# Another order for the first steps of a gated-recurrence and SiLU-layer kernel on one core

## The chip, the cores and the metric

The kernel runs on one core of a Trainium2 chip. The metric is device time in microseconds (us) of one execution. The core has a matrix engine (PE; its weight loads are listed as PEld), three engines for elementwise work (DVE, the vector engine; ACT, the scalar engine; POOL, the general one) and SP, which here only sends DMA requests. Each engine runs its own instructions in the order of the program. Requests can also be sent from ACT and POOL. In the profile, SPq, ACTq and POOLq are these requests.

## The reference

Four sequences of 768 tokens, 8 heads of 48 values. Each head keeps a 48 x 48 state, which decays by a gate and takes up one outer product per token. All heads of a token together (384 values) then go through a layer of 2048 hidden values with SiLU.

```python
f = 1.0 / (1.0 + np.exp(-f_logit))
for t in range(S):
    state = f[:, :, t, :, None] * state + np.einsum('bhd,bhe->bhde', k[:, :, t], v[:, :, t])
    y[:, :, t] = np.einsum('bhd,bhde->bhe', q[:, :, t], state)
x = y.transpose(0, 2, 1, 3).reshape(B * S, H * D)
h = x @ w_in
out = (h * (1.0 / (1.0 + np.exp(-h)))) @ w_out
```

q, k, v and f_logit come in float32, [4, 8, 768, 48]; w_in is [384, 2048] and w_out [2048, 384].

## The kernel before

A sequence is cut into 6 chunks of 128 tokens. Within a chunk the recurrence becomes matrix products: the logarithms of the gates are summed along the tokens, q and k are scaled by exponentials of these sums, their products (scores) are masked and multiplied with v, and the state from the chunk before is added. Two chunks make a *pair*, which shares its loads and its pass through the SiLU layer. Pairs 0 to 3 hold the first two chunks of sequences 0 to 3 (form "T", with even and odd tokens interleaved); pairs 4 to 11 hold the later chunks.

There is no loop over the pairs. A string, `PLAN` (lines 39 to 105), lists all steps as `name.pair.part:engine:buffers`, and lines 483 to 487 emit them in that order. Each engine so works through its own steps in the order of the string and waits where an input or a buffer isn't ready. Buffers are numbered by hand: a step that takes a buffer waits until the last reader of what was in it is done. The names, with the lines that emit them:

- `f`, `k`, `q`, `v` (line 228): a load of 384 KB, or two of 192 KB as for `f.1`.
- `E` (234) and `L` (238): exponential and logarithm of the gates of a pair, on ACT.
- `cs` (305, 309): sums of the logarithms along the tokens, on PE. Those of part 1 end with eight small products (309) for the decay of the state.
- `ia`, `a` (317): the two exponentials that scale k and q, on ACT; `al` (256): the decay of the state.
- `ki`, `qg` (322): k and q times these, on DVE (V) or POOL (G).
- `tq` (329) and `qkc` (184, 182): transposes on PE, and their copy out of PSUM.
- `sc` (346) and `at` (354): scores, and their masking on DVE.
- `vb`: v cast to bf16. `d` (275), `sd`, `su` (393): the new state; `su` is on POOL.
- `y` (263), `yi` (362), `yc`, `yT` (374), `xc`: the output, its copy, its transpose and the copy into the layer's input.
- `mi` (249), `si` (254), `mo` (286), `oc`, `so`: first product, SiLU, second product, copy out, store. One `mi` is six products of 256 columns, one `mo` step four of 384.
- `wi` (207), `wo` (210): a quarter of w_in or w_out, requested from POOL and cast on its way.
- `idle.N.K` (436): K products of a zeroed tile, N columns each. Nothing reads them.

Ahead of the plan's other steps lines 454 to 457 put the first four loads, and then ACT's first table load:

```python
        loads = [t for t in plan if t[0] in SRC][:4]
        for t in loads:
            run(*t)
        nc.scalar.preload_act_table_set(TABLES["exp"])
```

Before, these four are `f.1.0`, `f.1.1`, `f.0.0` and `k.1.0`. `f.1.1` is the one load of the opening that is sent from ACT. Pair 1 goes first, pair 0 second, and their `mi` and `mo` steps follow; pair 2's recurrence is worked in between the `mo` steps.

Of the kernel before, what the change touches and what calls it, by code (L numbers as in the profile page):

```python
# [36 lines left out]


PLAN = """
f.1.0:S:0 f.1.1:A: E.1.0:A:0 L.1.0:A:0 idle.512.10::0 cs.1.1:P:0 f.0.0:S:1 E.0.0:A:1 k.1.0:S:0 L.0.0:A:1 idle.512.1::1 cs.1.0:P:1  # L40
q.1.0:S:0 idle.512.2::2 cs.0.0:P:2 idle.256.1::3 cs.0.1:P:3 a.1.1:A:0 qg.1.1:V:0 a.1.0:A:1 ia.1.1:A:2 ki.1.1:V: idle.512.1::4 tq.1.1:P:4 ia.1.0:A:3
ki.1.0:V:1 v.1.0:S:0 f.2.0:S:0 qg.1.0:V: idle.512.3::5 tq.1.0:P:1 vb.1.1:V:0 vb.1.0:G:1 d.1:P:5,6 qkc.1.1:V:0 qkc.1.0:V: idle.512.1::7 idle.256.1::7
sc.1.0:P:1,4 ia.0.0:A:0 k.0.0:S:1 ki.0.0:V:0 at.1.0.0:V:0 at.1.0.1:V: idle.512.2::7 idle.256.1::7 sc.1.1:P:7,1 at.1.1.0:V:1 at.1.1.1:V: a.0.1:A:2
ia.0.1:A:3 sd.1.0:A:0 wi.1:G: al.1:A:0 E.2.0:A:1 L.2.0:A:1 q.0.0:S:1 a.0.0:A:1 qg.0.0:V: idle.512.1::5 cs.2.0:P:0 cs.2.1:P:5 al.2:A:1 ia.2.1:A:0
su.1.0:G:0 ia.2.0:A:4 al.0:A:2 a.2.0:A:1 qg.0.1:V:1 idle.512.2::2 y.1:P:1,7 tq.0.0:P:4 v.0.0:S:1 yc.1.0:V:0 a.2.1:A:2 qkc.0.0:A:1 sd.1.1:V:0 wi.3:G:
ki.0.1:G: tq.0.1:P:3 qkc.0.1:V: yT.1.0:P:1 yi.1.1:P: yc.1.1:A:0 wi.0:G: idle.512.2::2 sc.0.1:P:3,4 vb.0.1:G:0 at.0.1.0:V:0 yT.1.1:P:7 xc.1.0:A:0
sc.0.0:P:6,5 at.0.0.1:V:1 at.0.0.0:V: vb.0.0:A:1 wi.2:G: idle.512.1::2 d.0:P:3,1 xc.1.1:A: sd.0.0:A:1 su.0.0:G:0 mi.1.2:P:7 mi.1.3:P:3 at.0.1.1:V:
y.0:P:4,6 q.2.0:S:0 yc.0.0:A:0 yi.0.1:P: wo.0:G: mi.1.6:P:5 yT.0.0:P:4 sd.0.1:V:1 su.0.1:G:0 xc.0.0:A:1 wo.1:G: yc.0.1:V:1 yT.0.1:P:6 xc.0.1:V:
qg.2.1:G:0 mi.1.7:P:1 k.2.0:S:0 si.1.7:A:0 mi.0.3:P:6 mi.0.7:P:4 wo.2:G: si.1.6:A: mi.0.6:P:0 mi.0.1:P:1 si.0.1:A:1 wo.3:G: su.1.1:G:0 si.0.6:A:
mi.0.0:P:5 mi.0.2:P:2 si.0.2:A: mi.1.0:P:1 ki.2.1:V: si.1.3:A: mi.1.4:P:0 si.1.4:A: si.0.0:A: si.1.2:A: mi.0.5:P:2 mi.1.5:P:3 si.0.5:A: mi.0.4:P:0  # L50
mi.1.1:P:7 mo.0.1.0:P:2 v.2.0:S:0 si.1.5:A: mo.0.0.0:P:3 si.1.0:A: si.1.1:A: mo.1.0.0:P:7 mo.1.1.0:P:1 mo.1.0.1:P: mo.1.1.1:P: qg.2.0:V:1 f.3.0:S:0
si.0.3:A: mo.0.1.1:P: si.0.7:A: ki.2.0:V: tq.2.0:P:4 qkc.2.0:V:1 tq.2.1:P:6 mo.0.0.1:P: si.0.4:A: qkc.2.1:V: mo.1.1.2:P: sc.2.1:P:6,4 sc.2.0:P:0,5
at.2.0.0:V:0 at.2.0.1:V: mo.1.0.2:P: mo.0.0.2:P: at.2.1.0:V:1 at.2.1.1:V: mo.0.1.2:P: mo.0.1.3:P: vb.2.0:G:0 vb.2.1:A:1 d.2:P:6,5 sd.2.0:V:0 E.3.0:A:1
L.3.0:A:1 y.2:P:4,0 mo.1.1.3:P: oc.0.1:V:0 mo.0.0.3:P: cs.3.0:P:2 f.5.0:S:1 E.5.0:A:0 L.5.0:A:0 yc.2.0:V:1 a.3.0:A:4 su.2.0:G:0 sd.2.1:V:0 q.5.0:S:0
yi.2.1:P: yc.2.1:A:0 yT.2.0:P:4 cs.3.1:P:6 al.3:A:0 ia.3.1:A:1 cs.5.0:P:5 xc.2.0:V:0 a.5.0:A:0 cs.5.1:P:0 k.3.0:S:0 ki.3.1:G:0 yT.2.1:P:4 xc.2.1:V:
oc.0.0:A:1 q.3.0:S:1 mo.1.0.3:P: oc.1.0:A:2 oc.1.1:V:3 qg.3.0:V:1 mi.2.6:P:4 al.5.1:A:2 qg.5.0:V:2 k.5.1:S:1 a.5.1:A:1 mi.2.0:P:1 mi.2.1:P:7
mi.2.2:P:3 q.5.1:S: qg.5.1:V:3 ia.5.1:A:2 al.5.0:A:3 a.3.1:A:4 qg.3.1:V: k.5.0:S: ia.5.0:A:0 ki.5.1:G: v.3.0:S:0 ia.3.0:A:1 ki.3.0:V: mi.2.5:P:5
tq.3.1:P:2 qkc.3.1:V:1 si.2.1:A:0 ki.5.0:G: si.2.2:A: si.2.0:A: su.2.1:G:0 mi.2.3:P:6 tq.3.0:P:0 si.2.3:A: mi.2.4:P:2 qkc.3.0:V: mi.2.7:P:1
mo.2.1.0:P:6 mo.2.1.1:P: vb.3.1:G:0 si.2.4:A: vb.3.0:V:1 d.3:P:2,0 sd.3.0:V:0 su.3.0:G:0 si.2.5:A: v.5.0:S:1 si.2.6:A: sc.3.1:P:4,5 sc.3.0:P:3,7
at.3.0.0:V:0 si.2.7:A: mo.2.1.2:P: mo.2.1.3:P: vb.5.0:G:2 at.3.1.0:V:1 mo.2.0.0:P:3 mo.2.0.1:P: mo.2.0.2:P: f.4.0:S:1 E.4.0:A:0 sd.3.1:V:0 f.6.0:S:0  # L60
qkD.5.1:S:0 at.3.1.1:V: qkD.5.0:S:1 oc.2.1:A:4 L.4.0:A:0 cs.4.1:P:5 E.6.0:A:1 L.6.0:A:1 at.3.0.1:V: v.5.1:S: sc.5.0:P:7,6 y.3:P:0,4 sc.5.1:P:2,1
# [456 lines left out]
```

## Time and profile before

| | us |
|---|---|
| device time, median of three runs | 177.55 (177.32 to 177.99) |
| span of the profiled execution | 175.6 |
| first `mi` of the layer begins | 19.41 |

The time of the profiled execution is known by its span alone, from the first to the last instruction; it lies 1.95 us under the median of the three runs, which have the start and the end of an execution in them too. Times in views are counted from the start of the span. In a row of the timeline stand the start, the time from the first start to the last end of the group, the engine, the line, the operation with output and input, the count, and in brackets the idle time ahead of it with what ended it. Matmuls are pipelined: a group of them lasts longer than the time until the next one can begin.

### The profile page before, as it was taken

What the parts mean: (1) busy time and instruction counts of PE and PEld (TensorE: products, weight loads), DVE (VectorE), ACT (ScalarE), POOL (GpSimd) and SP (SyncE); (2) the same over time, 40 slices, a digit from 0 to 9 for tenths busy, and PEclk for the clock granted to TensorE, in tenths of its full rate; (3) what the DMA queues carried; (4) which work ended last, traced back from release to release, by engine and by line L of the source; (5) the groups of instructions that cost most, each with busy time, mean ns of one, the idle gap of its engine ahead of it and who ended that gap; (6) DMA issues with size and microseconds to landing.
All of it is one profiled execution on the core that took longest, in us unless ns stands there. A gap on an engine that the chain in (4) does not pass through costs nothing.

```text
span 175.6 us, 4754 instructions
## 1 busy us (share of the span) xinstructions
PE 169.4 (96%) x1927; PEld 125.2 (71%) x1930; DVE 81.2 (46%) x166; ACT 129.8 (74%) x239; POOL 61.2 (35%) x104
## 2 busy tenths in 40 slices
PE   6889999999999999999999999999999999999992
...
GB/s 146 320 325 265 211 216 201 188 182 240 232 172 164 210 208 158 228 183 217 128 230 166 143 236 158 205 188 231 225 128 183 193 191 230 54 61 118 90 4 90
DMA packets 110677, 32.12 MB, mean 183 GB/s; under 512 B 104096, under 2 KB 110528, under 8 KB 110656
## 3 DMA queue, kind: packets, MB, share of 16 engines
...
## 4 chain that ended last, share of the span: by engine, by line
PE 79%; ACT 11%; DVE 5%; DMA 2%; issue 2%
PE pb L286 35%; PE pb L249 29%; ACT x L317 3%; ACT hT L254 3%; PE pb L350 3%; ACT L485 2%; DVE qk L322 2%; DMA f<-in_f_logit_dram 2%; PE pb L362 2%; PE pb L366 2%; PE pb L346 1%; PE pb L312 1%; PE pb L383 1%; PE pb L374 1%; DVE atm L354 1%
## 5 line engine op out<-in xcount | busy, mean ns | idle before, releaser
L249 PE MATMUL pb<-xT,w_in_sb 128*128 128x256 bf16 x576 | 69.1, 272 | 0.3 <-ACT hT L254 0.2
L286 PE MATMUL pb<-w_out_sb,hT 128*128 128x384 bf16 (+2 forms) x400 | 68.6, 320 | 0.0
L249 PEld LDWEIGHTS <-w_in_sb 128*128 128x128 bf16 x576 | 54.8, 98 | 9.0 <-issue 0.8
L254 ACT ACTIVATE hT<-pb 128x512 bf16<-128x512 f32 x96 | 50.5, 611 | 10.9 <-PE pb L249 10.7
L286 PEld LDWEIGHTS <-hT 128*128 128x128 bf16 x400 | 37.2, 98 | 20.5 <-issue 0.2
L393 POOL TENSOR_TENSOR st<-sd,al 48x192 bf16<-48x192 f32 x40 | 21.4, 535 | 59.0 <-PE pb L362 33.4
L354 DVE TENSOR_TENSOR atm<-pb,triu 128x512 bf16<-128x512 f32 x32 | 20.1, 684 | 11.2 <-PE pb L350 6.6
L317 ACT ACTIVATE x<-pb 128x384 f32<-128x384 f32 x48 | 21.0, 501 | 5.4 <-PE pb L305 3.0
L485 ACT ACT_TABLE_LOAD x17 | 21.8, 1283 | 0.3
L184 DVE COPY ob<-pb 128x384 f32<-128x384 f32 (+1 forms) x11 | 5.7, 528 | 27.3 <-PE pb L286 27.3
L387 DVE TENSOR_TENSOR sd<-pb,st 128x384 f32<-128x384 f32 x16 | 8.8, 552 | 11.8 <-PE pb L383 10.3
L322 POOL TENSOR_TENSOR qk<-q,x 128x384 bf16<-128x384 f32 x11 | 10.9, 996 | 9.0 <-ACT x L317 6.1
L322 POOL TENSOR_TENSOR qk<-k,x 128x384 bf16<-128x384 f32 x11 | 11.8, 1081 | 5.7 <-ACT x L317 2.4
L182 ACT COPY ob<-pb 128x384 f32<-128x384 f32 (+1 forms) x14 | 6.7, 477 | 8.5 <-PE pb L286 8.1
L234 ACT ACTIVATE e<-f 128x768 f32<-128x768 f32 x12 | 10.1, 840 | 3.8 <-DMA f<-in_f_logit_dram 3.7
L322 DVE TENSOR_TENSOR qk<-q,x 128x384 bf16<-128x384 f32 x13 | 8.2, 648 | 7.2 <-ACT x L317 7.1
L354 DVE TENSOR_TENSOR atm<-pb,mask 128x512 bf16<-128x512 f32 x16 | 10.1, 684 | 1.6 <-issue 1.0
L436 PE MATMUL pb<-zero,triu 128*128 128x512 bf16 (+1 forms) x26 | 9.0, 449 | 1.4 <-POOL triu masks.py:66 1.4
L184 DVE CAST yb<-pb 128x384 bf16<-128x384 f32 x14 | 7.6, 554 | 5.1 <-PE pb L366 2.6
L184 DVE COPY qkTT<-pb 128x1024 bf16<-128x1024 bf16 x7 | 4.6, 683 | 11.0 <-PE pb L329 11.0
L322 DVE TENSOR_TENSOR qk<-k,x 128x384 bf16<-128x384 f32 x13 | 9.0, 707 | 1.0 <-DMA k<-in_k_dram 0.8
L184 POOL CAST vb<-v 128x384 bf16<-128x384 f32 x12 | 6.4, 535 | 8.0 <-DMA v<-in_v_dram 7.7
...
## 6 DMA issues: line engine op xcount, KB each, us to landing
f<-in_f_logit_dram SPq DMA_DIRECT2D x11, 384.0 KB, 5.1
k<-in_k_dram SPq DMA_DIRECT2D x10, 384.0 KB, 5.5
q<-in_q_dram SPq DMA_DIRECT2D x10, 384.0 KB, 5.4
v<-in_v_dram SPq DMA_DIRECT2D x10, 384.0 KB, 4.9
...
w_in_sb<-in_moe_w_in_dram POOLq DMA_DIRECT2D x4, 384.0 KB, 8.6
w_out_sb<-in_moe_w_out_dram POOLq DMA_DIRECT2D x4, 384.0 KB, 10.5
...
```

The lines of the kernel that those rows point to most:

```text
L184: ENG[eng].tensor_copy(dst, src)
L234: return nc.scalar.activation(e, at("f", P)[:, j * w:(j + 1) * w], AF.Exp, scale=-1.0)
L249: nc.tensor.matmul(h[:, i, cols], w_in_sb[:, kk, n * 128:(n + 1) * 128], at("xT", P)[:, kk, cols], start=(kk == 0), stop=(kk == KT - 1))
L254: return nc.scalar.activation(at("hT", P)[:, 2 * j:2 * j + 2, :], at("h", P, j).rearrange("p (n c) -> p n c", n=2), AF.Silu)
L286: nc.tensor.matmul(at("o" + key, P, i)[:, 0:cols.stop - cols.start], at("hT", P)[:, n, i * C:(i + 1) * C], w_out_sb[:, n, cols], start=(n ...
L317: nc.scalar.activation(at(kind, P, i).rearrange("p h d -> p (h d)"), at("cs", P, i)[:, 0:HD], AF.Exp, scale=1.0 if kind == "ia" else -1.0)
L322: ENG[eng].tensor_mul(at("qk", P, i)[:, j, :, 0:D], heads("qk"[j], P, i), at("ia" if j else "a", P, i))
L354: ENG[eng].tensor_mul(at("atm", P, i)[:, r], at(f"s{r}", P, i).rearrange("p (n c) -> p n c", c=C), mask[:, None, :].to_broadcast([C, NP, C]))
L387: nc.vector.tensor_add(at("sd", P, i), d_ps, prev_state(P, i))
L393: nc.gpsimd.tensor_mul(at("st", P, i)[lo:lo + D, :, r * D:(r + 1) * D], at("sd", P, i)[lo:lo + D, :, r * D:(r + 1) * D], al_of(P, i)[lo:lo ...
L436: nc.tensor.matmul(buf["pb", int(got)][:, 0:rest[0]], triu, zero[:, 0:rest[0]], start=True, stop=True, skip_group_check=True)
L485: nc.scalar.preload_act_table_set(turns[n])
```

## The change

Only the string is changed; every step is still there, with the same operands. Up to `cs.3.0` the order, some engines and many buffer numbers are others; behind it the order is as it was but for `k.3.0`, `su.0.1` and a few buffers. Three numbers count for all of the opening: the fillers before are ten of 512 columns at the very start and 16 more in thirteen places; after it there are seven and a half behind `cs.1.1`, a half one ahead of `sc.1.0` and ten behind `sc.1.1`.

```diff
-f.1.0:S:0 f.1.1:A: E.1.0:A:0 L.1.0:A:0 idle.512.10::0 cs.1.1:P:0 f.0.0:S:1 E.0.0:A:1 k.1.0:S:0 L.0.0:A:1 idle.512.1::1 cs.1.0:P:1
-q.1.0:S:0 idle.512.2::2 cs.0.0:P:2 idle.256.1::3 cs.0.1:P:3 a.1.1:A:0 qg.1.1:V:0 a.1.0:A:1 ia.1.1:A:2 ki.1.1:V: idle.512.1::4 tq.1.1:P:4 ia.1.0:A:3
-ki.1.0:V:1 v.1.0:S:0 f.2.0:S:0 qg.1.0:V: idle.512.3::5 tq.1.0:P:1 vb.1.1:V:0 vb.1.0:G:1 d.1:P:5,6 qkc.1.1:V:0 qkc.1.0:V: idle.512.1::7 idle.256.1::7
-sc.1.0:P:1,4 ia.0.0:A:0 k.0.0:S:1 ki.0.0:V:0 at.1.0.0:V:0 at.1.0.1:V: idle.512.2::7 idle.256.1::7 sc.1.1:P:7,1 at.1.1.0:V:1 at.1.1.1:V: a.0.1:A:2
-ia.0.1:A:3 sd.1.0:A:0 wi.1:G: al.1:A:0 E.2.0:A:1 L.2.0:A:1 q.0.0:S:1 a.0.0:A:1 qg.0.0:V: idle.512.1::5 cs.2.0:P:0 cs.2.1:P:5 al.2:A:1 ia.2.1:A:0
-su.1.0:G:0 ia.2.0:A:4 al.0:A:2 a.2.0:A:1 qg.0.1:V:1 idle.512.2::2 y.1:P:1,7 tq.0.0:P:4 v.0.0:S:1 yc.1.0:V:0 a.2.1:A:2 qkc.0.0:A:1 sd.1.1:V:0 wi.3:G:
-ki.0.1:G: tq.0.1:P:3 qkc.0.1:V: yT.1.0:P:1 yi.1.1:P: yc.1.1:A:0 wi.0:G: idle.512.2::2 sc.0.1:P:3,4 vb.0.1:G:0 at.0.1.0:V:0 yT.1.1:P:7 xc.1.0:A:0
-sc.0.0:P:6,5 at.0.0.1:V:1 at.0.0.0:V: vb.0.0:A:1 wi.2:G: idle.512.1::2 d.0:P:3,1 xc.1.1:A: sd.0.0:A:1 su.0.0:G:0 mi.1.2:P:7 mi.1.3:P:3 at.0.1.1:V:
-y.0:P:4,6 q.2.0:S:0 yc.0.0:A:0 yi.0.1:P: wo.0:G: mi.1.6:P:5 yT.0.0:P:4 sd.0.1:V:1 su.0.1:G:0 xc.0.0:A:1 wo.1:G: yc.0.1:V:1 yT.0.1:P:6 xc.0.1:V:
-qg.2.1:G:0 mi.1.7:P:1 k.2.0:S:0 si.1.7:A:0 mi.0.3:P:6 mi.0.7:P:4 wo.2:G: si.1.6:A: mi.0.6:P:0 mi.0.1:P:1 si.0.1:A:1 wo.3:G: su.1.1:G:0 si.0.6:A:
...
+f.1.0:S:0 f.0.0:S:2 k.1.0:S:0 q.1.0:S:1 f.1.1:A: E.1.0:A:0 L.1.0:A:2 cs.1.0:P:1 E.0.0:A:0 ia.1.0:A:2 v.1.0:S:5 k.0.0:S:3 cs.1.1:P:4 f.2.0:S:0
+ki.1.0:V:3 ia.1.1:A:3 a.1.1:A:4 L.0.0:A:2 al.1:A:3 a.1.0:A:2 ki.1.1:V:4 idle.512.7::0 idle.256.1::0 cs.0.0:P:0 vb.1.0:G:2 qg.1.1:V: tq.1.1:P:2
+q.0.0:S:0 cs.0.1:P:1 a.0.0:A:3 ia.0.0:A:4 vb.1.1:A:1 al.0:A:4 qg.1.0:V: qkc.1.1:V:0 tq.1.0:P:7 d.1:P:4,0 qkc.1.0:V: idle.256.1::3 sc.1.0:P:3,2 wi.1:G:
+ki.0.0:V:3 sc.1.1:P:7,5 a.0.1:A:0 sd.1.0:A:0 at.1.0.1:V:1 at.1.0.0:V: idle.512.10::6 at.1.1.0:V:2 ia.0.1:A:4 at.1.1.1:V: E.2.0:A:0 L.2.0:A:0
+cs.2.1:P:3 wi.3:G: qg.0.0:V: su.1.0:G:0 a.2.1:A:1 sd.1.1:V:0 wi.0:G: al.2:A:0 ia.2.1:A:3 y.1:P:1,6 yi.1.1:P: tq.0.0:P:5 cs.2.0:P:2 ki.0.1:G:2
+qg.0.1:G: tq.0.1:P:4 yc.1.1:A:1 v.0.0:S:2 yc.1.0:V:0 yT.1.0:P:0 vb.0.1:G:5 qkc.0.0:V:0 vb.0.0:G:1 yT.1.1:P:6 wi.2:G: wo.0:G: ia.2.0:A:4 a.2.0:A:0
+d.0:P:3,7 xc.1.1:A:1 qkc.0.1:V: xc.1.0:V: sc.0.1:P:5,2 at.0.1.0:V:3 sc.0.0:P:6,1 sd.0.0:A:1 at.0.0.1:V:2 su.0.0:G:0 mi.1.3:P:4 mi.1.2:P:5 mi.1.6:P:0
+mi.1.7:P:3 at.0.1.1:V: at.0.0.0:V: y.0:P:1,2 yi.0.1:P: sd.0.1:V:1 yc.0.1:V:0 q.2.0:S:0 si.1.6:A:0 mi.1.0:P:6 k.2.0:S:0 yc.0.0:A:2 yT.0.0:P:1
+xc.0.0:A:2 f.3.0:S:0 yT.0.1:P:0 xc.0.1:V: si.1.7:A: mi.1.1:P:2 qg.2.0:G:2 qg.2.1:G:1 v.2.0:S:3 mi.0.2:P:7 mi.0.0:P:0 ki.2.1:V: si.1.3:A: si.1.1:A:
+mi.0.6:P:1 si.0.0:A:2 si.1.2:A: wo.1:G: si.0.2:A: mi.0.1:P:3 si.0.1:A: mi.0.5:P:2 mi.0.7:P:4 si.0.6:A: si.0.7:A: si.1.0:A: si.0.5:A: mi.0.4:P:3
+mi.0.3:P:1 mi.1.4:P:5 mo.0.1.0:P:4 wo.2:G: si.0.4:A: wo.3:G: si.1.4:A: tq.2.1:P:6 mo.1.1.0:P:7 ki.2.0:V: tq.2.0:P:2 mo.1.0.0:P:3 si.0.3:A: mi.1.5:P:5
...
+mo.1.1.2:P: cs.3.0:P:2 f.5.0:S:0 E.5.0:A:0 L.5.0:A:0 yc.2.0:V:1 a.3.0:A:4 mo.0.1.3:P: mo.1.1.3:P: oc.0.1:V:0 mo.0.0.3:P: su.2.0:G:0 sd.2.1:V:0
```

What it does to each engine's own order:

- **First loads.** The first four loads of the string are now `f.1.0`, `f.0.0`, `k.1.0` and `q.1.0`, all sent from SP. `f.1.1` is the fifth, so ACT's program has the table load ahead of it.
- **ACT.** `ia.1.0`, `ia.1.1` and `a.1.1` come ahead of `L.0.0`; before, `E.0.0` and `L.0.0` came first. `vb.1.1` comes to ACT from DVE, and `qkc.0.0`, `vb.0.0` and `xc.1.0` leave ACT.
- **PE.** `cs.1.0` and `cs.1.1` come first, with no filler ahead of them. Two half-pairs of scores (`sc.1.0` and `sc.1.1`) stand beside each other, and four `mi` steps ahead of `y.0` where there were two.
- **POOL.** `wi.1` and `wi.3` are requested together ahead of `su.1.0`; `qg.0.1` and `vb.0.0` come to POOL; both halves of `qg.2` stand ahead of `wo.1`; `su.0.1` moves behind `ki.5.1`.
- **SP.** `q.2.0` takes the buffer of `q.0.0` and so waits for `qg.0.0` and `qg.0.1`; `k.2.0`, `f.3.0` and all later loads stand behind it. `f.5.0` takes the buffer of `f.3.0` and waits for `E.3.0`.

More of the change, by code (lines that the diff above doesn't have):

```diff
@@ L48 @@
-y.0:P:4,6 q.2.0:S:0 yc.0.0:A:0 yi.0.1:P: wo.0:G: mi.1.6:P:5 yT.0.0:P:4 sd.0.1:V:1 su.0.1:G:0 xc.0.0:A:1 wo.1:G: yc.0.1:V:1 yT.0.1:P:6 xc.0.1:V:
-qg.2.1:G:0 mi.1.7:P:1 k.2.0:S:0 si.1.7:A:0 mi.0.3:P:6 mi.0.7:P:4 wo.2:G: si.1.6:A: mi.0.6:P:0 mi.0.1:P:1 si.0.1:A:1 wo.3:G: su.1.1:G:0 si.0.6:A:
-mi.0.0:P:5 mi.0.2:P:2 si.0.2:A: mi.1.0:P:1 ki.2.1:V: si.1.3:A: mi.1.4:P:0 si.1.4:A: si.0.0:A: si.1.2:A: mi.0.5:P:2 mi.1.5:P:3 si.0.5:A: mi.0.4:P:0
-mi.1.1:P:7 mo.0.1.0:P:2 v.2.0:S:0 si.1.5:A: mo.0.0.0:P:3 si.1.0:A: si.1.1:A: mo.1.0.0:P:7 mo.1.1.0:P:1 mo.1.0.1:P: mo.1.1.1:P: qg.2.0:V:1 f.3.0:S:0
@@ L52 @@
[L52 to L55, printed above, removed]
```

13 lines of the change are left out of this document (8 added, 5 removed).

## The prediction, made ahead of the result

> **What bounds the kernel now.** I read the page first: the share of each engine, the slices, the chain that ended last.
>
> ```profile
> span 175.6 us, 4754 instructions
> PE 169.4 (96%) x1927; PEld 125.2 (71%) x1930; DVE 81.2 (46%) x166; ACT 129.8 (74%) x239; POOL 61.2 (35%) x104
> PE   6889999999999999999999999999999999999992
> PE 79%; ACT 11%; DVE 5%; DMA 2%; issue 2%
> ```
>
> PE is busy nearly everywhere and carries 79% of the chain; only the first slices are thinner. So I asked for the busy time by stages, and for the chain in order of time.
>
> ```profile
> 22.40:31.00 8.60, 8.60 (x83) 7.67 (x82) 2.58 (x4) 7.41 (x13) 5.37 (x9) 1.00 1.22 207
> 36.00:43.00 7.00, 7.00 (x123) 4.55 (x121) 5.01 (x9) 2.69 (x4) 0.53 (x2) 1.00 0.99 217
> ...
> 0.74 3.44 DMA f<-in_f_logit_dram
> 19.48 1.42 PE pb L249 x12
> 22.67 8.52 PE pb L249 x78
> 31.19 4.55 PE pb L286 x28
> ```
>
> From 22.4 us PE is full (8.60 of 8.60, then 7.00 of 7.00), and 13 `mi` steps (78 products in 8.52) make 0.655 each, without a gap. What PE has left from the first `mi` on is the same before and after: no product moves from one side of that point to the other. The end therefore moves by as much as the `mi` steps move, unless a gap opens later. The question is when PE comes to them.
>
> **The opening, term by term.** The timeline of the first microseconds has the durations.
>
> ```profile
> 0.74 0.47 ACTq L228 DMA_DIRECT2D f<-in_f_logit_dram  x1
> 0.74 1.00 SPq L228 DMA_DIRECT2D f<-in_f_logit_dram  x2
> 1.25 1.28 ACT L457 ACT_TABLE_LOAD   x1 [1.25 <-PEq L502]
> 1.37 4.07 PE L436 MATMUL pb<-zero,triu 128*128 128x512 bf16 x10 [1.37 <-POOL triu masks.py:66]
> 4.20 0.84 ACT L234 ACTIVATE e<-f 128x768 f32<-128x768 f32 x1 [1.67 <-DMA f<-in_f_logit_dram]
> 4.33 0.15 PEld L436 LDWEIGHTS <-triu 128*128 128x128 bf16 x1 [0.28 <-issue]
> 4.76 0.15 PEld L436 LDWEIGHTS <-triu 128*128 128x128 bf16 x1 [0.28 <-issue]
> 5.06 0.10 PEld L305 LDWEIGHTS <-tincl 128*128 128x128 bf16 x1 [0.15 <-issue]
> 5.08 0.84 ACT L238 ACTIVATE lf<-e 128x768 bf16<-128x768 f32 x1
> 5.97 0.48 PE L305 MATMUL pb<-lf,tincl 128*128 128x384 bf16 x2 [0.53 <-ACT lf L238]
> 6.29 0.34 PE L309 MATMUL pb<-halves,lf 128*128 128x2 bf16 x8
> 7.03 0.59 PE L436 MATMUL pb<-zero,triu 128*128 128x512 bf16 x2
> 7.43 2.41 ACT L317 ACTIVATE x<-pb 128x384 f32<-128x384 f32 x6
> 9.08 0.54 POOL L184 CAST vb<-v 128x384 bf16<-128x384 f32 x1 [5.17 <-DMA v<-in_v_dram]
> 9.56 0.91 POOL L207 DMA_DIRECT2D w_in_sb<-in_moe_w_in_dram  x1
> 10.55 0.62 PE L329 MATMUL pb<-ident,qk 128*128 128x128 bf16 x8 [0.41 <-ACT x L317]
> 10.69 1.28 DVE L184 COPY qkTT<-pb 128x1024 bf16<-128x1024 bf16 x2
> 12.48 2.48 DVE L354 TENSOR_TENSOR atm<-pb,mask 128x512 bf16<-128x512 f32 x4
> ```
>
> *`f.1.1`.* `E.1.0` needs both halves of `f.1`. The ACT half was requested at 0.74 and ended the wait at 4.20; the table load followed the request. Now the table load comes first. Bounds: the request goes out at about 0.8, if only the instruction stream is held, or at 0.74 + 1.28 = 2.02, if it waits for the table load to end; then all of the opening is 1.28 later. No row shows an ACT request behind unrelated ACT work. A POOL request waited so: `wi.1`, which needs nothing from `vb.1.0`, began at 9.56, as that copy ended at 9.62. But a POOL request takes 0.91 where ACT's took 0.47 and SP's 0.50 each, and SP has no datapath to wait for: ACT's is nearer to SP's. I take 0.8, so `E.1.0` at 4.20 as before, and keep 2.02 as a rival. The Trainium skill (Perfetto Trace Analysis, "DVE / Act Engine Instruction") says that the sequencer is free for the next instruction once it has pushed an ACT one into its wait queue. No row here tests that; by it the sum would be the one I take.
>
> *Decays first.* `L.1.0` ends at 5.92 as before. `E.0.0` now shares the buffer of `E.1.0` and runs from 5.95 to 6.8. The three exponentials ahead of `L.0.0` save pair 1 at most one logarithm, 0.84.
>
> *PE starts at half speed.* The ten fillers began 0.43 apart (weight loads at 4.33 and 4.76), two later ones 0.21 apart (0.59 less one's 0.38); the change came by 5.06, 3.7 after PE's first work. Without them `cs.1.0` is PE's first work, at 5.97, and by the same interval PE is slow until 9.65. `cs.1.0` and `cs.1.1` take 4 x 0.32 in place of 4 x 0.16. The eight small products hold PE 0.2 at full speed (6.29 to the next filler at 6.49); slow, between 0.4 (twice) and 1.2 (eight slow weight loads of 0.15), I take 0.6, nearer to the row that has just these. PE is through at 5.97 + 1.28 + 0.6 = 7.85. `ia.1.1` begins at about 8.1, `a.1.1` ends at 9.0, `L.0.0` at 9.75: the 0.84 is mostly spent on the wait for `cs.1.1`.
>
> *The fillers stand in line.* Seven and a half begin at 7.85: until 9.65 4.2 of them, then 3.3 x 0.21 = 0.7, to 10.35. `cs.0.0` (2 x 0.16), `tq.1.1` (0.45 until the next may begin), `cs.0.1` (0.32 + 0.2) and `tq.1.0` (0.62) end at 12.25; their inputs are there by then. Before, `tq.1.0` ended at 11.17: **1.1 later**.
>
> *Masks.* `qkc.1.0` 0.68 and the four masks, 2.48, stay, and `ki.0.0` (0.55) stands between them as before. The masks end at 16.0, against 14.96: 1.0 later. The ten fillers behind `sc.1.1` fill PE until about 15.9 and take 2.1 beside these masks; they cost nothing as long as the masks end last.
>
> ```profile
> 12.30 1.08 POOL L393 TENSOR_TENSOR st<-sd,al 48x192 bf16<-48x192 f32 x2 [1.83 <-ACT al L256]
> 13.33 0.81 POOL L207 DMA_DIRECT2D w_in_sb<-in_moe_w_in_dram  x1
> 14.21 0.99 POOL L322 TENSOR_TENSOR qk<-k,x 128x384 bf16<-128x384 f32 x1
> 15.24 0.58 PE L263 MATMUL pb<-vb,atm 64*128 64x48 bf16 x32
> 16.51 1.07 ACT L182 COPY qkTT<-pb 128x1024 bf16<-128x1024 bf16 x1
> 18.96 0.37 PEld L275 LDWEIGHTS <-qk 64*128 64x128 bf16 x16 [0.23 <-DVE atm L354]
> ```
>
> *From the masks to the first `mi`.* Before, this took 19.41 - 14.96 = 4.45: ACT's slow `qkc.0.0` (1.07) and three copies behind it held `d.0` until 18.96. Now these are spread over DVE and POOL. Two strings are left. On PE: `cs.2.1` 0.52 after the fillers, `y.1` 0.4, `yi.1.1` 0.2, `tq.0.0` 0.45, `cs.2.0` 0.32, `tq.0.1` 0.62, to 18.4. On POOL: `su.1.0` from 13.4 (1.08), the request `wi.0` 0.8, `ki.0.1` and `qg.0.1` 0.99 each, to 17.3, so inside the first. Then `qkc.0.1` 0.68 and the scores of pair 0, 0.44: `mi.1.3` begins at 19.55. The stretch is 0.9 shorter, against masks 1.0 later: **+0.15**.
>
> *The first `mi` steps.* Three steps took 22.67 - 19.41 = 3.26 with `y.0` and the transposes among them, where the work is 3.1: `y.0` had waited for the last mask. With four `mi` steps ahead of `y.0` (2.6) the masks of pair 0 (2.48) are hidden: **-0.15**. If they weren't, it would cost what is left of them, about 0.2.
>
> ```profile
> q<-in_q_dram SPq DMA_DIRECT2D x1, 384.0 KB, 7.8
> w_out_sb<-in_moe_w_out_dram POOLq DMA_DIRECT2D x1, 384.0 KB, 10.4
> ...
> 23.00 0.80 POOL L210 DMA_DIRECT2D w_out_sb<-in_moe_w_out_dram  x1
> 39.06 0.84 ACT L234 ACTIVATE e<-f 128x768 f32<-128x768 f32 x1 [2.03 <-DMA f<-in_f_logit_dram]
> 43.82 0.49 ACT L317 ACTIVATE x<-pb 128x384 f32<-128x384 f32 x1 [3.04 <-PE pb L305]
> ```
>
> *Transfers.* The first two rows are of the view of the DMAs; their last number is the time from request to landing, here of `q.2.0` and `wo.1`. `q.2.0` (7.8 to land) now goes out behind `qg.0.1`, near 17.4, and lands between 22 and 25. Nothing of pair 2 is wanted before `tq.2.1`, near 32. But `wo.1` now waits on POOL behind both `qg.2`: requested at 25 to 27 where it was at 23.00, it lands, at 10.4 or less, by 37.4 at the latest, and the fifth `mo`, right behind pair 2's scores, wants it near 36. I take nothing for it, as less traffic is in flight, and keep 1.5 as its price. `f.5.0` waits for `E.3.0` now; ACT had 3.04 spare ahead of `a.3.0`. `su.0.1` adds 1.08 to POOL near 48, ahead of `ki.5.0`, whose scores come ten microseconds later. I cost both at nothing.
>
> Sum: +0.15 - 0.15, and 0.1 for the waits between engines that I rounded away: 175.7 against the profiled 175.6. On the median of 177.55 that is **177.65**, no change.
>
> **The rivals.**
>
> *The request waits for the table load.* For it speaks `wi.1`; against it ACT's short request. All steps follow `E.1.0`, so 1.28 is added: **178.95**, slower. It decides from the point where `f.1.1`'s landing passes 4.2 by more than 0.8.
>
> *PE wakes late.* One interval, 3.7, is one sample. If PE is still slow at the end of the fillers, these take 0.5 longer, and `cs.0.0` to `tq.1.0` (1.9) up to as much again. The middle is 0.9: **178.55**. For it speaks that `cs.1.1` uses PE thinly; against it that ten plain fillers needed no more than 3.7. The Trainium skill (TensorE: Matmul & The Clock Gate, "What's actually happening") has a rule against this change: the clock opens after a busy window of 3413 ns that runs freely, not from the first product. As an estimate from that page, PE would open 3.4 to 6.8 after its start, and the middle, 5.1, would make the sum some 0.9 longer; the row's 3.7 lies inside.
>
> *The relief is larger than its price.* If PE is awake at `cs.1.0`, or the fillers end sooner, `tq.1.0` can end at 11.2 as before, and the shorter stretch of 3.55 behind the masks is a gain of 0.9 to 1.1: **176.55**. Against it stands that nothing runs on PE in its first 6 us.
>
> *`wo.1` is late*, as priced: **179.15**.
>
> **How the numbers follow.** My forecast 0.40, the request behind the table load 0.28, late waking 0.12, the larger relief 0.12, late `wo.1` 0.08. The forecast's own range is 177.1 to 178.3. The whole range, 176.8 to 179.4, takes in the table-load case and half of the others' tails. Half a per cent, 0.9, is about what a measurement of this kernel can tell from no change. Faster by more: most of the relief, 0.11. Slower: most of the table-load case and of late `wo.1`, half of late waking, 0.40. Within it: 0.49.
>
> **What would show it.** In the trace after, the ACT request begins at 0.8 (or at 2.0); `E.1.0` starts at 4.2 (5.5); the fillers behind `cs.1.1` run 0.43 apart and end near 10.4 (10.9 or more if PE wakes late); the masks of pair 1 end at 16.0; the first `mi` begins at 19.55, and PE shows no gap from there to 43. A gap ahead of an `mo` with a DMA as its releaser, or a first `mi` before 18.7 or after 20.4, would make the prediction wrong.

## The result and the profile after

Over 20 runs each, the changed kernel has a median of 178.62 us (177.15 to 179.81), the kernel before 177.26 (177.13 to 178.47). The ratio is 1.0058, with a 95% interval of 1.004 to 1.0075: slower, clear of noise, and just beyond the half per cent up to which the forecast called it no change. Ratios leave out the runs in which the chip was in a slower state; medians and ranges have all runs in them. 177.65 was forecast, within a range of 176.8 to 179.4; the range held, the likeliest case was about a microsecond too fast. Against its own base the miss is larger: the forecast added 0.1 to 177.55, the median of three runs, and the 20 runs of the kernel before have 177.26. The profiled execution had a span of 176.1, where the one before had 175.6. It took 177.90, so a time lies 1.8 above its span.

The page of the changed kernel, the lines that were shown of before:

```profile
span 176.1 us, 4727 instructions
PE 166.7 (95%) x1920; PEld 124.9 (71%) x1920; DVE 80.5 (46%) x165; ACT 129.3 (73%) x238; POOL 64.2 (36%) x106
PE   0699999999999999999999999999999999999992
PEclk9999999999999999999999999999999999999999
PE 88%; ACT 7%; DMA 2%; DVE 1%; issue 1%; ACTq 0%
```

Only the first three slices of PE differ: 0, 6 and 9 instead of 6, 8 and 8. PE's share of the chain has grown from 79% to 88%, which doesn't mean that PE does more, but that it now holds the opening too. The timeline of the opening (start, time, engine, line, operation, count, wait in brackets):

```profile
0.74 1.28 ACT L456 ACT_TABLE_LOAD   x1 [0.74 <-PEq L501]
0.77 0.48 ACTq L227 DMA_DIRECT2D f<-in_f_logit_dram  x1
4.27 0.84 ACT L233 ACTIVATE e<-f 128x768 f32<-128x768 f32 x1 [2.25 <-DMA f<-in_f_logit_dram]
6.04 0.48 PE L304 MATMUL pb<-lf,tincl 128*128 128x384 bf16 x1 [6.04 <-ACT lf L237]
7.53 3.36 PE L435 MATMUL pb<-zero,triu 128*128 128x512 bf16 x8
10.68 0.40 PE L304 MATMUL pb<-lf,tincl 128*128 128x384 bf16 x1
10.92 0.33 PE L304 MATMUL pb<-lf,tstrict 128*128 128x384 bf16 x1
12.06 0.61 PE L328 MATMUL pb<-ident,qk 128*128 128x128 bf16 x8
13.92 2.48 DVE L353 TENSOR_TENSOR atm<-pb,mask 128x512 bf16<-128x512 f32 x4
...
18.70 0.50 PE L373 MATMUL pb<-ident,yb 128*128 128x128 bf16 x6
19.13 0.51 PE L274 MATMUL pb<-vb,qk 64*128 64x96 bf16 x16
19.64 0.64 PE L345 MATMUL pb<-qkTT 48*64 48x128 bf16 x32
20.21 2.79 PE L248 MATMUL pb<-xT,w_in_sb 128*128 128x256 bf16 x24
```

How to read it: the request on ACT went out at 0.77, beside the table load that ran from 0.74 to 2.02. The Trainium skill (Perfetto Trace Analysis, "DVE / Act Engine Instruction") has the sequencer free for the next instruction once it has pushed one into the wait queue; this row agrees. All eight fillers of 7.53 ran at half speed (3.36 together, 0.43 apart); a sum of 384 columns took 0.48 at 6.04, 0.40 at 10.68 and 0.33 at 10.92, so PE reached full speed near 10.8. `tq.1.0` ended at 12.67, the masks at 16.40, and the first `mi` began at 20.21, 0.80 later than before (19.41). In the windows after it (us, PE's busy time with its count, granted clock, DMA share, GB/s), PE is as full as before, and nothing that was moved on the queues shows:

```profile
22.40:31.00 8.60, 8.60 (x113) 1.00 1.19 208
36.00:43.00 7.00, 7.00 (x93) 1.00 0.75 160
```

Of the 0.80, 0.5 is left at the end of the span (176.1 - 175.6); 0.13 of the rest is that PE rests less between 22 and 125 us (table below).

### The profile page after: what moved, and what is told of

It reads as the page before. It is cut to its first block, busy times and chain, and to the rows that moved or that the text cites. A ratio compares the mean times of both kernels' runs of the same rounds, so it can differ in the third digit from the quotient of the medians.

```text
span 176.1 us, 4727 instructions
## 1 busy us (share of the span) xinstructions
PE 166.7 (95%) x1920; PEld 124.9 (71%) x1920; DVE 80.5 (46%) x165; ACT 129.3 (73%) x238; POOL 64.2 (36%) x106
## 3 DMA queue, kind: packets, MB, share of 16 engines
q0 software_dynamic: 3936, 3.74, 12.4%
## 4 chain that ended last, share of the span: by engine, by line
PE 88%; ACT 7%; DMA 2%; DVE 1%; issue 1%; ACTq 0%
PE pb L285 35%; PE pb L248 31%; PE pb L435 3%; ACT hT L253 3%; PE pb L349 3%; PE pb L361 2%; ACT L484 2%; PE pb L328 2%; PE pb L304 2%; DMA f<-in_f_logit_dram 2%; PE pb L365 2%; PE pb L311 2%; PE pb L373 1%; PE pb L345 1%; PE pb L382 1%; PE pb L262 1%
## 5 line engine op out<-in xcount | busy, mean ns | idle before, releaser
L392 POOL TENSOR_TENSOR st<-sd,al 48x192 bf16<-48x192 f32 x40 | 22.2, 555 | 57.0 <-PE pb L361 33.8
L321 POOL TENSOR_TENSOR qk<-q,x 128x384 bf16<-128x384 f32 x13 | 13.5, 1047 | 9.7 <-DMA q<-in_q_dram 5.4
L386 DVE TENSOR_TENSOR sd<-pb,st 128x384 f32<-128x384 f32 x16 | 8.7, 551 | 10.8 <-PE pb L382 10.0
L321 DVE TENSOR_TENSOR qk<-k,x 128x384 bf16<-128x384 f32 x13 | 8.1, 638 | 4.7 <-ACT x L316 3.4
L304 PE MATMUL pb<-lf,tincl 128*128 128x384 bf16 x12 | 3.8, 379 | 6.0 <-ACT lf L237 6.0
L183 DVE COPY qkTT<-pb 128x1024 bf16<-128x1024 bf16 x8 | 5.5, 692 | 8.3 <-ACT hT L253 5.6
L181 ACT CAST yb<-pb 128x384 bf16<-128x384 f32 x10 | 4.8, 490 | 5.7 <-PE pb L365 3.7
L321 DVE TENSOR_TENSOR qk<-q,x 128x384 bf16<-128x384 f32 x11 | 7.1, 656 | 3.0 <-ACT x L316 2.9
## 6 DMA issues: line engine op xcount, KB each, us to landing
w_out_sb<-in_moe_w_out_dram POOLq DMA_DIRECT2D x4, 384.0 KB, 10.4
```

Of the source, the lines that this page charges most:

```text
L181: nc.scalar.copy(dst, src)
L183: ENG[eng].tensor_copy(dst, src)
L321: ENG[eng].tensor_mul(at("qk", P, i)[:, j, :, 0:D], heads("qk"[j], P, i), at("ia" if j else "a", P, i))
L386: nc.vector.tensor_add(at("sd", P, i), d_ps, prev_state(P, i))
L392: nc.gpsimd.tensor_mul(at("st", P, i)[lo:lo + D, :, r * D:(r + 1) * D], at("sd", P, i)[lo:lo + D, :, r * D:(r + 1) * D], al_of(P, i)[lo:lo ...
```

## The experiments

Two theories stood at the start. CLOCK: the change takes away the ten fillers with which PE came to full speed while ACT still computed the first gates; now PE does its first real work at half speed. GATE: a microsecond won or lost in the opening need not reach the end, since later PE waits for something with a time of its own. RELIEF and ORDER ask what the moves between the engines, and the order of the steps, are worth; what ORDER means differs from text to text and is said in each.

All runs in one table. "Full speed" is the time from PE's first product to its full speed, read from the durations (a filler 0.43 or 0.21 apart, a weight load 0.15 or 0.10). "Rests" is PE's idle time from 22 to 125 us. The remainder is the span less the first `mi` and less the rests. Each ratio is to the kernel before on the same chip.

| kernel | full speed after | first `mi` | rests | span | remainder | median | ratio (interval) |
|---|---|---|---|---|---|---|---|
| before | 3.6 | 19.41 | 0.34 | 175.6 | 155.9 | 177.26 | |
| after | 4.8 | 20.21 | 0.21 | 176.1 | 155.7 | 178.62 | 1.0058 (1.004 to 1.0075) |
| before_no_front | 3.1 | 19.94 | 0.32 | 175.9 | 155.6 | 178.32 | 1.0042 (1.0014 to 1.0069) |
| front_fillers | 2.9 | 18.27 | 2.68 | 176.9 | 156.0 | 178.82 | 1.0064 (1.004 to 1.0088) |
| no_middle_fillers | 6.4 | 20.21 | 0.23 | 176.4 | 156.0 | 178.24 | 1.0047 (1.0035 to 1.0059) |
| front_no_middle | 5.1 | 18.35 | 0.52 | 175.0 | 156.1 | 177.18 | 0.999 (0.9964 to 1.0015) |
| after_early_k8 | 4.8 | 20.15 | 0.20 | 176.1 | 155.8 | 178.06 | 1.005 (1.0032 to 1.0068) |
| front_early_k8 | 4.0 to 4.5 | 18.10 | 1.46 | 175.5 | 155.9 | 177.08 | 0.9977 (0.9955 to 0.9998) |
| front_no_middle_early_k8 | 4.0 to 4.6 | 19.42 | 0.82 | 176.1 | 155.9 | 177.59 | 0.9992 (0.9965 to 1.0018) |
| before_early_k8 | 3.5 | 19.35 | 0.31 | 175.3 | 155.6 | 177.72 | 1.0031 (1.0011 to 1.0052) |
| relief_undone | 6.1 | 21.64 | 0.23 | 177.8 | 155.9 | 178.71 | 1.0089 (1.0074 to 1.0104) |
| q2_in_free_buffer | 4.9 | 20.24 | 0.20 | 176.2 | 155.8 | 178.08 | 1.0046 (1.0032 to 1.006) |
| front_store_on_pool | 6.0 | 18.71 | 1.04 | 175.8 | 156.0 | 176.82 | 0.9982 (0.9965 to 0.9999) |
| front_log_first | 4.8 | 18.81 | 0.53 | 175.2 | 155.9 | 177.06 | 0.9989 (0.9973 to 1.0006) |

The remainder is 155.6 to 156.1 in all fourteen traces: two numbers, the first `mi` and PE's later rests, account for a span to within a quarter of a microsecond. The median of the kernel before was 177.1 to 177.4 beside the experiments, so the ratios compare better than the medians.

**The first fillers put back, and taken from before.** `front_fillers` is the changed kernel with ten fillers at the very start:

```diff
-f.1.0:S:0 f.0.0:S:2 k.1.0:S:0
+idle.512.10::0 f.1.0:S:0 f.0.0:S:2 k.1.0:S:0
```

> The changed kernel with ten fillers of 512 columns put back at its very start, all else as changed. Theory CLOCK (the loss and the spread of the changed kernel come from PE being at half speed from 6.0 us until a moment that differs from run to run): fillers begin near 1.4 us, PE is at full speed by 6 us, cs.1.1 ends near 6.7, the 7.5 fillers behind it run 0.21 apart, tq.1.0 ends near 11 (12.67 in the profile of the changed kernel), the first mi begins near 18.5, device time about 176.3 with a spread under 0.6. Theory ORDER (the new order costs by itself, through POOL's longer string and the wait of q.2.0): first mi stays near 20, device time stays at 177.9 to 178.6.

`before_no_front` is the kernel before without its ten:

```diff
-L.1.0:A:0 idle.512.10::0 cs.1.1:P:0
+L.1.0:A:0 cs.1.1:P:0
```

> The kernel before without its ten first fillers, all else as before. CLOCK: PE's first work is cs.1.1 at 6.0 at half speed; the fillers and sums between it and tq.1.1 take twice as long, tq.1.1 begins 1 to 2.5 us later than 8.75, device time 178 to 179.5 with a spread of 1.5 or more. ORDER: the ten fillers do nothing that the kernel needs, so the time stays at 177.3 with a spread of about 0.5.

Three rows of the timeline of `before_no_front`:

```profile
5.90 0.80 PE L305 MATMUL pb<-lf,tincl 128*128 128x384 bf16 x2 [5.90 <-ACT lf L238]
10.01 0.61 PE L329 MATMUL pb<-ident,qk 128*128 128x128 bf16 x8
19.94 1.49 PE L249 MATMUL pb<-xT,w_in_sb 128*128 128x256 bf16 x12
```

The first sums take 0.80 where they took 0.48, `tq.1.1` begins at 10.01 instead of 8.75, and the first `mi` 0.53 later than before.

The timeline of `front_fillers`, PE and the masks:

```profile
1.37 3.66 PE L435 MATMUL pb<-zero,triu 128*128 128x512 bf16 x10 [1.37 <-POOL triu masks.py:66]
6.91 1.78 PE L435 MATMUL pb<-zero,triu 128*128 128x512 bf16 x8
10.11 0.61 PE L328 MATMUL pb<-ident,qk 128*128 128x128 bf16 x8
...
11.97 2.49 DVE L353 TENSOR_TENSOR atm<-pb,mask 128x512 bf16<-128x512 f32 x4
```

The eight fillers behind `cs.1.1` now take 1.78 instead of 3.36, `tq.1.0` ends at 10.72 instead of 12.67, and the first `mi` comes 1.94 sooner than in the changed kernel and 1.14 sooner than before. Taking the ten from before alone gives a ratio of 1.0042, which the interval can't tell from the whole change's 1.0058. At the first `mi`, both directions bear CLOCK out. In the device time the table has two more pairs that differ by the first fillers alone, each pair on one chip: `after_early_k8` and `front_early_k8` (1.005 and 0.9977), `no_middle_fillers` and `front_no_middle` (1.0047 and 0.999). In both the intervals lie apart: the fillers that the change dropped carry its loss.

The spread is another matter. CLOCK expected it to fall under 0.6 in `front_fillers`, and even the nine runs that its ratio is taken from spread over 2.2 us; in `before_no_front` it expected 1.5 or more, and it is 1.3.

But `front_fillers` isn't faster at the end (1.0064), because PE rests 2.48 of the 25 us behind 100. Its windows, its waits of PE (in total, times, longest), the timeline of DVE, and the chain there:

```profile
100.00:125.00 25.00, 22.52 (x233) 1.00 0.93 186
```

```profile
PE pb L285 <- DVE yb L183: 1.8, 1, 1.8
...
PE pb L349 <- DMA qkT<-qk: 0.7, 1, 0.7
```

```profile
106.58 0.56 DVE L321 TENSOR_TENSOR qk<-k,x 128x384 bf16<-128x384 f32 x1 [3.52 <-DMA k<-in_k_dram]
107.05 1.01 DVE L183 CAST yb<-pb 128x384 bf16<-128x384 f32 x2
```

```profile
99.81 6.68 DMA k<-in_k_dram
```

PE's `mo` waits for a PSUM buffer, which two copies on DVE (`yc.7.1`, `yc.7.0`) free; these stand on DVE behind `ki.8.0`, and `ki.8.0` waits 3.52 for the load `k.8.0`. The engine that PE waits for isn't the cause: the load behind it is. SP's requests tell why it is late. Before, SP sent `qkD.7.1` (line 337) at 97.48 and this load's group at 98.79:

```profile
97.48 1.26 SPq L337 DMA_TRANSPOSE qkT<-qk  x1
98.79 2.24 SPq L228 DMA_DIRECT2D k<-in_k_dram  x2
```

And in `front_fillers`:

```profile
97.89 1.24 SPq L336 DMA_TRANSPOSE qkT<-qk  x1
99.17 2.08 SPq L227 DMA_DIRECT2D k<-in_k_dram  x2
```

They went out no sooner, although PE had begun its `mi` 1.14 sooner. From 58.81 to 94.60 SP's requests stand one behind another in this trace, with pauses of at most 0.12, so SP was behind and an earlier PE ran into it. That is GATE. It isn't a fixed time: in `front_no_middle`, whose first `mi` is as early (18.35), the same two requests left at 96.87 and 98.16, and PE rests 0.52 in all. What decides between the two isn't shown.

**The fillers in the middle.** `no_middle_fillers` is the changed kernel, `front_no_middle` is `front_fillers`, each with this edit:

```diff
-ki.1.1:V:4 idle.512.7::0 idle.256.1::0 cs.0.0:P:0
+ki.1.1:V:4 cs.0.0:P:0
```

> The changed kernel without the 7.5 fillers behind cs.1.1. If these fillers stand in line for nothing, cs.0.0 begins near 9.4 in place of 10.7 and the time falls by up to 0.7 to about 177.3. CLOCK says more: PE rests from 7.5 to 9.3, so it wakes later (after 13), and sums, transposes, scores behind it run at half speed; 178 to 180, a spread of 1.5 or more remains. ORDER: 177.3 to 178, small spread.

> Ten fillers at the very start, and none of the 7.5 behind cs.1.1. CLOCK: PE is awake at 6 us and stays so (the rest between cs.1.1 and cs.0.0 is under 2 us); cs.0.0 begins when L.0.0 ends near 8.9, with or without the fillers, so within 0.4 us of the run with both, about 176.2, spread under 0.6. If the 7.5 fillers are what keeps PE at full speed, it comes out slower than that run by 0.5 or more and spreads.

```profile
9.30 0.48 PE L304 MATMUL pb<-lf,tincl 128*128 128x384 bf16 x1 [1.69 <-ACT lf L237]
```

This row is of `no_middle_fillers`. Without them, `cs.0.0` began at 9.30 instead of 10.68, but PE stayed slow until about 12.4, and the first `mi` began at 20.21, as in the changed kernel. In these two traces, what the fillers cost in line they gave back by waking PE sooner. The median of 178.24 is as CLOCK expected, the spread of 0.24 in five runs isn't (1.5 or more). With the fillers in front, leaving out those in the middle moved the first `mi` by 0.08 (18.35). The time was expected near that of `front_fillers`; its ratio is lower (0.999 instead of 1.0064), and so are PE's rests (0.52 instead of 2.68).

**The late load.** `k.8.0` is moved ahead of three transposes and a load on SP (`qkD.7.0`, `yD.6.0`, `qkD.7.1` and `k.9.0`), in the changed kernel (`after_early_k8`), in `front_fillers` (`front_early_k8`), in `front_no_middle` (`front_no_middle_early_k8`) and in the kernel before (`before_early_k8`):

```diff
-mo.4.1.3:P: qkD.7.0:S:0 oc.4.0:A:3
+mo.4.1.3:P: k.8.0:S:0 qkD.7.0:S:0 oc.4.0:A:3
...
-k.9.0:S:1 k.8.0:S:0 sc.7.1:P:6,7
+k.9.0:S:1 sc.7.1:P:6,7
```

> The changed kernel with the load k.8.0 sent ahead of both transposes qkD.7, one load and two transposes earlier on SP; the opening as changed. Theory GATE (a wait of DVE for k.8.0 near 105 us, with the copies that PE's mo steps need queued behind it, holds the time back and makes part of the spread): the wait of DVE for k.8.0 (0.4 us in the changed kernel's profile) is gone, the median falls by about 0.5 to some 178 and the spread to about 1.7, which is what PE's awakening alone leaves. Theory CLOCK ALONE: median 178.6 and spread 2.6 as before.

> Ten fillers at the start as in front_fillers, and k.8.0 early. GATE: front_fillers lost its 1.1 to 1.3 us of earlier mi steps to a 2.5 us wait near 106; without it the time is 176.1 to 176.4 with a spread under 0.7, below the kernel before. If the wait only moves to the next load or transpose, the time stays at 177 to 178.8.

> Ten fillers at the start, none behind cs.1.1, k.8.0 early. GATE: as front_early_k8, 176.1 to 176.4. If the middle fillers keep PE at full speed, slower than that run and spread over 1.

> The kernel before with k.8.0 early. GATE: PE waited there 0.15 us in the profile before, so 177.1 to 177.3, hardly a change from 177.3; the kernel before comes to that place late enough. If the early load itself gains or costs (the transposes behind it come 0.6 later), it shows here.

In `front_early_k8` the wait for `k.8.0` is gone and the ratio falls from 1.0064 to 0.9977. A part of the wait only moved: the chain now runs through the transpose `qkD.7.1`, sent at 98.36, and PE waits 1.0 ahead of `sc.7.1`.

```profile
98.36 3.23 DMA qkT<-qk
```

It was expected at 176.1 to 176.4 if the wait went; 177.08 fits the case that it moves.

In the changed kernel, whose PE is too late to meet the gate, the same edit took away DVE's wait of 0.44 for `k.8.0` and left the span at 176.1. The median of 178.06 and the range of 1.8 are as GATE expected, but the ratio's interval overlaps the changed kernel's. In the kernel before it was expected to change nothing, and it came out slower, by a ratio of 1.0031; no wait of PE in its trace shows why (0.2 in all from 60 to 125 us). The profiled execution, 177.12, is near the lowest of its twelve (177.05). That stays open.

`front_no_middle_early_k8` shows what the fillers in the middle may be for. A row of its timeline, and its windows (length, busy time of PE, weight loads, DVE, ACT and POOL with counts, granted clock, DMA share, GB/s):

```profile
8.75 0.32 PE L304 MATMUL pb<-lf,tincl 128*128 128x384 bf16 x1 [1.75 <-ACT lf L237]
```

```profile
7.00:9.00 2.00, 0.25 (x2) 0.18 (x2) 1.50 (x3) 2.00 (x6) 0.00 (x0) 1.00 1.17 325
9.00:11.00 2.00, 2.00 (x25) 1.60 (x24) 1.47 (x2) 1.63 (x6) 1.88 (x3) 0.57 1.17 325
11.00:13.00 2.00, 2.00 (x47) 1.44 (x49) 1.16 (x2) 0.93 (x3) 0.27 (x2) 0.57 1.17 323
```

PE rested 1.75 us ahead of 8.75, and from about 9.3 to 12.7 it was back at half speed, with a granted clock of 0.57. The first `mi` came at 19.42 instead of 18.35. In the profile of `front_no_middle` nothing of the kind followed a rest of 1.69. So half speed can follow such a rest, and doesn't always. That the rest is the cause isn't shown: the first products behind it, at 8.75, 8.91 and 9.07, still began 0.16 apart, which is full speed.

**The moves between the engines.** `relief_undone` is the changed kernel with `qkc.0.0`, `vb.0.0` and `xc.1.0` on ACT again:

```diff
-qkc.0.0:V:0 vb.0.0:G:1
+qkc.0.0:A:0 vb.0.0:A:1
...
-xc.1.0:V:0
+xc.1.0:A:0
```

> The changed kernel with three of its side-by-side moves put back: `qkc.0.0`, `vb.0.0` and `xc.1.0` run on ACT again, as they did before the change; the rest of the opening stays. RELIEF (these three are what shortens the stretch between the masks and the first `mi`): masks of pair 1 unchanged at 16.4, the first `mi` 0.5 to 0.9 us later than the changed kernel's 20.21, so 20.7 to 21.1; if that shift goes through to the end, 179.2 to 179.5. ORDER (the stretch is set by PE's own chain from `sc.1.x` to `d.1`, and ACT has room): first `mi` within 0.2 of 20.21 and the time within 0.4 of the changed kernel's 178.6. GATE (what the opening loses or gains is taken up between 60 and 110 us by the queue of loads): first `mi` as RELIEF says, but the time under 179.0.

The first `mi` came at 21.64, 1.43 later. Its timeline splits that: the masks began at 14.43 (13.92 in the changed kernel), and from their end to the first `mi` it took 4.73 (21.64 - 16.91) instead of 3.81 (20.21 - 16.40).

```profile
14.43 2.48 DVE L353 TENSOR_TENSOR atm<-pb,mask 128x512 bf16<-128x512 f32 x4
...
18.64 1.01 ACT L181 COPY qkTT<-pb 128x1024 bf16<-128x1024 bf16 x1
19.55 0.52 ACT L181 CAST vb<-v 128x384 bf16<-128x384 f32 x1
20.11 0.52 PE L274 MATMUL pb<-vb,qk 64*128 64x96 bf16 x16 [0.41 <-ACT vb L181]
```

The second part, 0.92, is RELIEF, just above what was expected: ACT's slow copy (1.01) and the cast behind it make `d.0` wait 0.41 at 20.11, and what follows waits too. The first part, 0.5, is another awakening: here PE stayed slow for 6.1 us. The ratio rises by 0.0031 over the changed kernel's, which is 0.55 us; the two intervals just touch. The median of 178.71 lies under RELIEF's 179.2 to 179.5, in GATE's range. But PE rests no longer than in the changed kernel (0.23 and 0.21), so the trace shows no gate; it is of the slowest of the six executions (179.62).

**The loads of pair 2.** `q2_in_free_buffer` has `q.2.0` in a buffer that nothing holds:

```diff
-q.2.0:S:0 si.1.6:A:0
+q.2.0:S:3 si.1.6:A:0
```

> The changed kernel with `q.2.0` loaded into buffer 3, which is free, instead of buffer 0, so that it and the loads of pair 2 behind it on SP no longer wait until `qg.0.x` has read buffer 0. LOADS FREE (the prediction's step 8: these transfers land long before they are used): `q.2.0` sent near 10 to 11 us instead of 17.93, opening unchanged (masks 16.4, first `mi` 20.2), time within 0.4 of the changed kernel's 178.6. CONTENTION (loads of pair 2 now share the 16 engines with `wi.1` and `wi.2`): first `mi` or the first `mo` later by 0.3 or more and a time of 179 or over. LOADS LATE (in the changed kernel the loads behind `q.2.0` are late after all): 178.2 or less.

The request went out at 10.25 instead of 17.93, and PE's marks didn't move: first `mi` 20.24, span 176.2. Its median of 178.08 lies in the range of LOADS LATE (178.2 or less), but the intervals of the ratios (1.0046 and 1.0058) overlap, and PE rests as long as in the changed kernel (0.20 and 0.21). The trace shows LOADS FREE; the time can't tell the two apart.

**A request less on SP.** `front_store_on_pool` is `front_early_k8` with one store sent from POOL:

```diff
-cs.8.1:P:4 so.3.1:S:
+cs.8.1:P:4 so.3.1:G:
```

> The variant with ten fillers at the very front and `k.8.0` asked for early (177.08), and in it the store `so.3.1` sent from POOL instead of SP, where it stood from 90.64 for 3.54 us. GATE BY SP (requests leave SP one after another, and one that waits for its data holds those behind it): the wait of PE for `qkT` before `sc.7.1`, 1.01 us in that variant, falls under 0.3, and the time to 176.0 to 176.5. GATE BY THE ENGINES (the 16 DMA engines are full between 60 and 110 us): the wait of PE near 106 us keeps 0.7 or more, and the time stays at 176.9 to 177.3. POOL LATE (the store holds POOL's own work back): a wait for POOL appears after 90 us and the time is 177.5 or more.

The chain at the place of the wait, two rows of SP's timeline, and behind them the request for `k.8.0` in `front_early_k8`:

```profile
98.57 3.26 DMA qkT<-qk
```

```profile
91.68 2.88 SPq L227 DMA_DIRECT2D k<-in_k_dram  x1
...
98.57 1.25 SPq L336 DMA_TRANSPOSE qkT<-qk  x1
```

```profile
94.23 0.59 SPq L227 DMA_DIRECT2D k<-in_k_dram  x1
```

Though 3.5 us of requests had left SP, the transpose went out at 98.57 instead of 98.36. SP was already 0.96 behind at the load ahead of this place (`f`, at 89.96 instead of 89.00), so it gained 0.75 of the 3.5 here. In the place of the store other requests took longer: `k.8.0`, 0.59 on SP in `front_early_k8`, now took 2.88. So SP's order isn't all that holds them. That speaks for full DMA engines, which one run doesn't prove. PE's wait ahead of `sc.7.1` fell under 0.3, as GATE BY SP expected, but a wait of 0.7 came up ahead of an `mi` at 100.61; the median of 176.82 lies between the two expectations.

**The decays first.** `front_log_first` is `front_fillers` with pair 0's logarithm ahead of pair 1's decays again:

```diff
-E.0.0:A:0 ia.1.0:A:2
+E.0.0:A:0 L.0.0:A:1 ia.1.0:A:2
...
-a.1.1:A:4 L.0.0:A:2 al.1:A:3
+a.1.1:A:4 al.1:A:3
```

> The variant with ten fillers at the very front, and in it `L.0.0` put back ahead of `ia.1.0`, so that pair 0's logarithm again runs before pair 1's decays; PE is at full speed from about 5 us. ORDER (decays first is worth what ACT saves, at most the 0.84 of the two waits): `a.1.0` 0.3 to 0.8 us later, and with it `tq.1.0`, masks (end 14.46 in the variant) and the first `mi` (18.27 there) 0.2 to 0.8 us later. FREE (the decays wait for `cs.1.1` in any case): first `mi` within 0.15 of 18.27. Under either, by GATE, the time stays within 0.5 of that variant's 178.8, since a delay under 1.9 us is taken up by PE's wait near 106 us.

```profile
9.67 0.62 PE L328 MATMUL pb<-ident,qk 128*128 128x128 bf16 x8 [0.64 <-DVE qk L321]
```

`tq.1.1` waits 0.64 for `qg` in this row of PE's timeline, the masks end at 15.00 instead of 14.46, and the first `mi` is 0.54 later: ORDER holds, and the decays first are worth 0.54 when PE is awake. But the time was expected to stay near 178.8, and it is 177.06. The request for `k.8.0` left at nearly the same time (98.93 and 99.17 for the two loads of `k`), and the load took 5.21 instead of 6.68, so `ki.8.0` waited 1.27 instead of 3.52:

```profile
99.57 5.21 DMA k<-in_k_dram
```

What sets these 5.2 or 6.7 us wasn't found. GATE is right that there is a gate; when it opens differed by more here than the 0.54 that the opening lost.

## Why the prediction was right in its range, and wrong in its likeliest case

1. *The ACT request* was forecast at 0.8 and `E.1.0` at 4.20; they came at 0.77 and 4.27. The rival with the request behind the table load, chance 0.28, is refuted.
2. *Decays first* "save pair 1 at most one logarithm", mostly spent. Right: the order is worth 0.54 with PE awake. In the changed kernel `tq` has no wait in brackets, so PE itself was late and the order couldn't help.
3. *"By the same interval PE is slow until 9.65"*: **this is the step that failed.** It was slow until about 10.8, 4.8 after its start instead of 3.7. The traces without a rest on the way have 2.9 to 6.1. One row was taken as a constant of the chip, and it is a sample. The small products of `cs.1.1` were the other way off: PE was through at 7.53, not 7.85.
4. *The fillers in line and `tq.1.0`*: 12.25 forecast, 12.67 measured. From the rows: -0.32 from `cs.1.1`, +0.65 since all fillers ran slow (3.15 from 7.53 to 10.68 instead of 2.5), +0.09 behind them.
5. *The masks* end at 16.40, not 16.0: the same 0.4.
6. *From the masks to the first `mi`*: 3.81, not 3.55. The mechanism, ACT's copies, is shown by `relief_undone` (0.92, where 0.9 was the forecast of the whole stretch). The size was off since PE's own string was added up without the transposes of 18.70 (0.43 until the next may begin) and without `d.0` (0.51): behind the masks PE never waited, so its own work was the bound, not DVE's copy.
7. *The first `mi` steps*, -0.15: didn't show. The end of three `mi` steps before was read from the chain, 22.67; the timeline has the next one begin at 22.51. So the steps took 3.10, the work itself, and there was nothing to gain; `y.0` had not waited for the last mask (its row, at 20.83, has no wait). The row of before's timeline:

```profile
22.51 4.75 PE L249 MATMUL pb<-xT,w_in_sb 128*128 128x256 bf16 x42
```

8. *Transfers*: right, by the full windows above and by `q2_in_free_buffer`. `wo.1` went out at 24.31, and PE had no gap from 36 to 43, so the rival with a late `wo.1` didn't come; nor did the larger relief.

The first `mi` was thus 0.66 later than forecast (0.4 by steps 3 and 4, 0.26 by step 6). The forecast span of 175.7 became 176.1. The rest of the difference, from 177.90 for the profiled execution to 178.62 for the median, lies in executions without a trace. The rival "PE wakes late", with a chance of 0.12, is what happened, at about half of its price: the fillers ended at 10.68, between the forecast's 10.4 and the rival's 10.9, and 0.4 of its 0.9 shows in the trace. That its 178.55 lies so near the median of 178.62 is luck in part. The page of the Trainium skill that was quoted for it (TensorE: Matmul & The Clock Gate, "What's actually happening": a busy window that runs freely) should have weighed more than one row. The estimate from it was 3.4 to 6.8 us; of the thirteen traces without a rest on the way eleven lie inside, and two under it (2.9 and 3.1).

Whether the clock explains the wider spread after (2.7 us between the lowest and the highest run, 1.3 before) isn't shown. Before, the slow time falls on fillers from 1.37 on; after, it falls on work. As an estimate, awakenings from 2.9 to 6.1 would make 1.6 us at half speed, so not all of 2.7. And `front_fillers` speaks against it, with 2.2 us although in its trace the slow time falls on fillers alone. The runs without a profile don't show their awakening; this stays open.

Of the versions tried, `front_early_k8` and `front_store_on_pool` lie under before by 0.2%, with intervals that end at 0.9998 and 0.9999. At the first `mi` the relief (0.92) and the order (0.54) are worth keeping, if the first fillers stay.
